# An expert layer with 624 instead of 640 static slots per expert

## The chip, the cores and the metric

The kernel runs on one core of one Trainium2 chip. The metric is the device time of one execution in microseconds, the median of repeated runs. Three timed runs of the kernel before gave 769.81, 770.02 and 771.15 us.

## The reference

Attention with rotary position embedding over 4 batches, 8 heads, 576 positions and 64 dimensions; its output, 2304 rows of 512, is the input of a layer of 8 experts. Each row goes to the two experts with the largest noisy logits and gets the weighted sum of their outputs:

```python
logits = x @ w_gate
noisy_logits = logits + np.log1p(np.exp(x @ w_noise)) * noise
top2 = np.argpartition(-noisy_logits, 2, axis=1)[:, :2]
# top2_w: softmax over the two
for e in range(E):
    for k in range(2):
        mask = top2[:, k] == e
        h = np.maximum(x[mask] @ w1[e], 0.0)          # 512 -> 1024
        out[mask] += top2_w[mask, k, None] * (h @ w2[e])   # 1024 -> 512
```

4608 assignments of rows to experts are made in all, 576 an expert on average; how many an expert gets depends on the data.

## The kernel before

Operations are not written out in their final order. `add` puts each one on a list with its engine, an estimated duration, its dependencies, the buffers that it takes and a priority; `Plan.order` (L199) simulates the engines with these numbers and fixes the order in which instructions are issued. `CFG["dp"]` holds one correction of priority for each operation, by its place in the list.

**Attention and routing** fill the first half. Routing ranks the experts of each token, counts, and scatters each row (512 values as an fp16 high and low part, the weights of the experts, the row numbers) into `xs_rows` in DRAM, which has a region of `REG` rows for each expert; unused slots hold padding whose row number is out of bounds. An expert has `CAP` static slots (L29), in `NJ = CAP // 128` tiles of 128. Experts 0 and 1 are worked on in two parts, slots 0 to 255 before the routing of the last rows is done, and the rest later (`EARLY`, L1164); experts 2 to 7 in one part (`FULL`).

**Each expert** runs through these steps.

- `load_x` (L1172): a transposed load on SyncE's queue brings the rows into `xt` (128 x 8 x slots, fp16: four blocks of 128 dimensions, high and low part), a second load brings `meta` (weights and row numbers), and VectorE scales the weights into `gsc`.
- `weights`, `plan_weights` (L1113, L1144): eight pieces of 512 KB of w1 and w2 are loaded through the staging buffer `wst` and cut into fp16 high and low parts by ScalarE and VectorE. w1 and w2 have two buffers each, for even and odd experts.
- `up` (L1210): for each of 8 blocks of 128 hidden units, 12 products (four blocks of dimensions, three pairs of high and low parts). A product takes one matmul of `w_` columns for a part of up to 512 slots, and two of half the slots (320) for 640. The weights are the stationary operand, `xt` is streamed. ScalarE writes the relu as fp16 (`hh`), VectorE the remainder (`hl`).
- `down` (L1278): for each tile of 128 slots, 24 matmuls of 512 columns (8 blocks of hidden units, three pairs of parts), with the slots as the stationary operand. VectorE scales the sum and adds `prev`, the rows of the output so far, which `fetch` (L1259) has gathered; `spread` (L1306) scatters the result into the output from GpSimd. Gathers of an expert wait for all scatters of the one before.

TensorE's order in the second half is, by and large: first the up blocks of the next expert's block 0, then the down tiles of this expert, then the other seven up blocks of the next one. All matmuls but a few are issued by the helper `mm`, so they carry its line L537 in the trace, and the tile names `ps` (up) and `dn` (down) tell them apart.

**Overflow.** `count` (L1323) compares the largest number of tokens of an expert with `CAP`. Behind the static program a branch handles what is over: it reloads that expert's weights (`reload`) and works on each further 128 slots with `more` (L1431), one step after the other.

Of the kernel before, what the change touches and what calls it, by code (L numbers as in the profile page):

```python
# [12 lines left out]
F16 = mybir.dt.float16  # L13
# [3 lines left out]
OP = mybir.AluOpType  # L17
# [4 lines left out]
NTOK, DM, NE, FF = B * S, 512, 8, 1024  # L22
# [3 lines left out]
QS, VS, XS, MC = 16.0, 64.0, 128.0, 64.0  # L26
PB = 12
GS, W1S, W2S = 256.0, 32.0, 32.0
CAP = 640  # L29
NJ = CAP // 128  # L30
REG = NTOK + CAP
ROW = 1024 + 20
FAR = 1 << 20

# [277 lines left out]
def build(ctx, tc, q, k, v, w_gate, w_noise, noise, w1, w2, tab_d, out):  # L312
    nc = tc.nc
    xs = nc.dram_tensor("xs_rows", (NE * REG, ROW // 2), I32, kind="Internal").ap()

# [10 lines left out]
    pools = {}  # L326
# [209 lines left out]
    def mm(o, w, m, first, last):  # L536
        nc.tensor.matmul(o, w, m, start=first, stop=last, skip_group_check=True)  # L537
# [290 lines left out]
    def masks2():  # L828
# [13 lines left out]
           op0=OP.mult, op1=OP.subtract), prio=25, deps=["wgh"])  # L842
# [45 lines left out]
    def ring(name, bufs):  # L888
        if name not in R_:
            R_[name] = Ring(name, bufs, lambda: None)  # L890
        return R_[name]
# [273 lines left out]
    FULL = ((0, CAP),)  # L1165

    def tiles_of(c0, c1):
        return range(c0 // 128, c1 // 128)

    xbuf, mbuf, gbuf, hbuf, pbuf, ybuf = {}, {}, {}, {}, {}, {}  # L1170

    def load_x(e, c0, c1, deps, pr):  # L1172
        def f():
            s = hid.setdefault(e, dict(meta={}, gsc={}, prev={}, adds=[]))
            if e == 0 and c0 == 0:
                xt = pools["r"].tile([128, 8, c1], F16, name="xe")
            else:
                if "xt" not in s:
                    s["xt"] = pools["l"].tile([128, 8, CAP], F16, name="xt", bufs=2)
                xt = s["xt"][:, :, c0:c1]  # L1180
            s["xt", c0] = xt
            rows = xs[e * REG + c0:e * REG + c1]
            nc.sync.dma_start_transpose(out=xt, in_=rows[:, 0:512].bitcast(F16))  # L1183
            n = (c1 - c0) // 128
            meta = pools["r"].tile([128, NJ, 10], I32, name="meta", bufs=4)
            nc.sync.dma_start(meta[:, 0:n], rows[:, 512:522].rearrange("(j p) m -> p j m", p=128))
            for j in tiles_of(c0, c1):
                s["meta"][j] = (meta, j - c0 // 128)

        def weigh():  # L1190
            s = hid[e]
            n = (c1 - c0) // 128
            meta = s["meta"][c0 // 128][0]
            gsc = pools["r"].tile([128, NJ], F32, name="gsc", bufs=4)
            nc.vector.tensor_scalar(gsc[:, 0:n], meta[:, 0:n, e].bitcast(F32), 1.0 / (XS * W1S * W2S), None, op0=OP.mult)
            for j in tiles_of(c0, c1):
                s["gsc"][j] = gsc[:, j - c0 // 128:j - c0 // 128 + 1]
        if e == 0 and c0 == 0:
            xbuf[e, c0] = Buf(ring("xe", 1))
        else:  # L1200
            if (e, "xt") not in xbuf:
                xbuf[e, "xt"] = Buf(ring("xt", 2))
            xbuf[e, c0] = xbuf[e, "xt"]
        mbuf[e, c0], gbuf[e, c0] = Buf(ring("meta", 4)), Buf(ring("gsc", 4))
        n = (c1 - c0) // 128
        add(("x", e, c0), "SP", 1.1 * n + .4, f, deps=deps + ["swap_right"] + ([] if e == 0 and c0 == 0 else ["swap_left"]),
            uses=[xbuf[e, c0], mbuf[e, c0]], prio=pr, land=1.25 * n + .2)
        add(("wei", e, c0), "DVE", .2, weigh, deps=[("x", e, c0)], uses=[mbuf[e, c0], gbuf[e, c0]], prio=pr + 3)

    def up(e, f, c0, c1, pr):  # L1210
        n = 2 if c1 - c0 > 512 else 1
        w_ = (c1 - c0) // n
        ps_ = Buf(bigs)

        def mms():
            s = hid[e]
            wh, wl = wt[e]["w1"]
            xt = s["xt", c0]
            ps = ps_().rearrange("p (a b) -> p a b", a=2)
            i = 0  # L1220
            for c in range(4):
                for w, x in ((wh, c), (wh, 4 + c), (wl, c)):
                    for a in range(n):
                        mm(ps[:, a, 0:w_], w[:, c, f * 128:(f + 1) * 128], xt[:, x, a * w_:(a + 1) * w_], i == 0, i == 11)
                    i += 1

        def cut(lo):
            s = hid[e]
            if "hh" not in s:
                hid_ = pools["l" if e % 2 else "r"].tile([128, 2, 8, CAP], F16, name="hid", bufs=1)  # L1230
                s["hh"], s["hl"] = hid_[:, 0], hid_[:, 1]
            ps = ps_().rearrange("p (a b) -> p a b", a=2)
            hh = s["hh"][:, f, c0:c1].rearrange("p (a b) -> p a b", a=n)
            if lo:
                hl = s["hl"][:, f, c0:c1].rearrange("p (a b) -> p a b", a=n)
                nc.vector.scalar_tensor_tensor(hl, ps[:, 0:n, 0:w_], 0.0, hh, op0=OP.max, op1=OP.subtract)  # L1236
            else:
                nc.scalar.activation(hh, ps[:, 0:n, 0:w_], AF.Relu)  # L1238
        if e not in hbuf:
            hbuf[e] = Buf(ring("hid%d" % (e % 2), 1))  # L1240
        w = c1 - c0
        a, d = {256: (.28, .33), 384: (.39, .47), 640: (.6, .74)}[w]
        add(("up", e, f, c0), "PE", 12 * w / 2400 + .06, mms, deps=[("x", e, c0)] + wdone[e, "w1"],
            uses=[xbuf[e, c0], wbuf[e, "w1"], ps_], prio=pr)
        add(("hh", e, f, c0), "ACT", a, lambda: cut(False), deps=[("up", e, f, c0)] + (["swap_left"] if e % 2 else ["swap_right"]),
            uses=[ps_, hbuf[e]], prio=pr)
        add(("hl", e, f, c0), "DVE", d, lambda: cut(True), deps=[("hh", e, f, c0)], uses=[ps_, hbuf[e]], prio=pr)

    def ids(e, j, a):
        meta, i = hid[e]["meta"][j]  # L1250
        return meta[:, i, 8 + a:9 + a]
# [24 lines left out]
    behind = [[]]  # L1276

    def down(e, j, pr, prev=True):  # L1278
        dn = Buf(ring("dn", 2), lambda: pools["acc"].tile([128, 512], F32, name="dn"))
        c0 = c_of(e, j)  # L1280

        def mms(part):
            s = hid[e]
            wh, wl = wt[e]["w2"]
            cs = slice(j * 128, j * 128 + 128)
            for f in range(4 * part, 4 * part + 4):
                for a, (h, w) in enumerate(((s["hh"], wh), (s["hh"], wl), (s["hl"], wh))):
                    mm(dn(), h[:, f, cs], w[:, f], f == a == 0, f == 7 and a == 2)
        for part in range(2):
            add(("dn", e, j, part), "PE", 2.59, lambda part=part: mms(part),  # L1290
                deps=[("hl", e, f, c0) for f in range(8)] + wdone[e, "w2"] + ["swap_left"] + ([("dn", e, j, 0)] if part else behind[0]),
                uses=[dn, hbuf[e], wbuf[e, "w2"]], prio=pr + part * .1)

        behind[0] = [("dn", e, j, 1)]
        yb = Buf(ring("y", 2))
        yt = {}

        def scale():
            s = hid[e]
            y = yt[0] = pools["l"].tile([128, 512], F32, name="y", bufs=2)  # L1300
            if prev:
                nc.vector.scalar_tensor_tensor(y, dn(), s["gsc"][j], s["prev"][j], op0=OP.mult, op1=OP.add)  # L1302
            else:
                nc.vector.tensor_scalar(y, dn(), s["gsc"][j], None, op0=OP.mult)

        def spread():  # L1306
            s = hid[e]
            nc.gpsimd.memset(spacer, 0.0)
            i = nc.gpsimd.indirect_dma_start(  # L1309
                out=out, out_offset=bass.IndirectOffsetOnAxis(ap=ids(e, j, 0), axis=0),  # L1310
                in_=yt[0], in_offset=None, bounds_check=NTOK - 1, oob_is_err=False)
            for p in s["adds"]:
                tc.declare_no_dep(i.ins, p, reason="a token has one slot in an expert")
            s["adds"].append(i.ins)
        add(("y", e, j), "DVE", .67, scale, deps=[("dn", e, j, 1), ("wei", e, c0), "swap_left"] + ([("fe", e, j)] if prev else []),
            uses=[dn, yb, gbuf[e, c0]] + ([pbuf[e, j]] if prev else []), prio=pr - 2)
        add(("sp", e, j), "POOL", 1.07, spread, deps=[("y", e, j)] + ([("zero", i) for i in range(18)] if e == 0 else []) +
            ([("sp", e - 1, i) for i in range(NJ)] if e and not (e == 1 and j < 2) else []),
            uses=[yb, mbuf[e, c0]], prio=pr - 2, land=1.4)
# [44 lines left out]
    def go(us):  # L1364
        clk[0] += us

    def ups(e, f):
        up(e, f, *(FULL[0] if e > 1 else EARLY[1]), clk[0])
        go(3.2 if e > 1 else 1.95)

    for f in range(8):
        ups(0, f)
# [113 lines left out]
    with tc.If(some > 0):  # L1486
        for e in range(NE):
            ne = nc.values_load(cnt[0:1, e:e + 1], min_val=0, max_val=NTOK)
            with tc.If(ne > CAP):
                nc.gpsimd.indirect_dma_start(  # L1490
                    out=xs, out_offset=bass.IndirectOffsetOnAxis(ap=cst["tail"][:, e:e + 1], axis=0),
                    in_=pad, in_offset=None)
# [44 lines left out]
```

## Time and profile before

| | |
|---|---|
| median of the timed runs | 770.02 us |
| span of the profiled execution | 772.6 us |
| TensorE (PE) busy | 723.6 us, 94% |
| TensorE weight loads (PEld), overlapping | 497.5 us |
| VectorE (DVE) busy | 415.1 us, 54% |
| ScalarE (ACT) busy | 286.5 us, 37% |
| GpSimd (POOL) busy | 363.9 us, 47% |

Busy time is the time in which at least one instruction of the engine was in work. A row of TensorE's timeline gives the start of the first and the extent of a run of matmuls; matmuls are pipelined, so what one costs is the distance from one start to the next, and a mean duration is longer than that. L12 is line 12 of the kernel. Attention and routing take the span to about 359 us, the experts the rest.

### The profile page before, as it was taken

How to read it: one execution, taken by the hardware profiler on the slowest of the kernel's cores; microseconds unless marked ns; L12 is line 12 of the kernel's file. 1: busy time of each engine (PE TensorE's matmuls, PEld its weight loads, DVE VectorE, ACT ScalarE, POOL GpSimd, SP SyncE). 2: the span in 40 equal slices, each digit the busy share in tenths (PEclk: the TensorE clock that was granted, in tenths of full speed). 3: DMA queues.
4: the chain of work that ended last, by engine and by line, in shares of the span. 5: the costliest groups of instructions: out<-in, count | busy, mean ns of one | idle time of the engine just before them, and what ended most of it. 6: DMA issues, size and time to landing. Idle time of an engine off the chain costs nothing.

```text
span 772.6 us, 18628 instructions
## 1 busy us (share of the span) xinstructions
PE 723.6 (94%) x8094; PEld 497.5 (64%) x8094; DVE 415.1 (54%) x649; ACT 286.5 (37%) x435; POOL 363.9 (47%) x317
## 2 busy tenths in 40 slices
PE   4899998999888899989999999999999999999995
PEld 3677777788777777878555567466475574664752
DVE  6758779877769778777224524334343352342211
ACT  2543546555554665764112313213223042140100
POOL 5799797996515697826431212240331222302311
PEclk9999999999799999999999999999999999999998
DMA  7786565957427594587744894645535537431201
GB/s 156 145 154 127 118 146 122 184 127 157 96 56 170 185 245 117 152 189 258 213 129 146 152 244 136 189 163 144 167 132 165 152 112 194 146 117 55 79 29 39
DMA packets 178812, 112.15 MB, mean 145 GB/s; under 512 B 150431, under 2 KB 155039, under 8 KB 178720
## 3 DMA queue, kind: packets, MB, share of 16 engines
q1 hardware_dynamic: 161632, 72.72, 42.8%
q0 software_dynamic: 9120, 29.03, 10.8%
q10 hardware_dynamic: 7968, 9.12, 3.5%
q8 instruction: 65, 1.06, 0.6%
q14 instruction: 27, 0.22, 0.1%
HBM read 58.57 MB, written 29.22 MB: 114 GB/s over the span
## 4 chain that ended last, share of the span: by engine, by line
PE 51%; issue 11%; DVE 5%; POOL 5%; ACT 4%; DMA 4%; SPq 1%; POOLq 0%; ACTq 0%; DVEq 0%
PE ps L537 25%; PE dn L537 20%; PE acc L537 6%; ACT p L662 2%; POOL p L673 2%; DVE nm L562 2%; POOL out_dram L1309 1%; DMA prev<-out_dram,meta 1%; DMA out_dram<-y,meta 1%; POOL prev L1263 1%; POOL xs_rows L1071 1%; ACT ps L662 1%; ACT xr L778 1%; SPq L1183 1%; DMA xs_rows<-xr,r_ii 1%
## 5 line engine op out<-in xcount | busy, mean ns | idle before, releaser
L537 PE MATMUL dn<-w2h,hid 128*128 128x512 f16 x640 | 191.8, 379 | 0.0
L537 PE MATMUL ps<-xt,w1h 128*128 128x320 f16 (+2 forms) x960 | 177.6, 301 | 0.3 <-DVE nf L1330 0.3
L1309 POOL DMA_INDIRECT out_dram<-y,meta x40 | 53.3, 1332 | 251.7 <-DVE y L1302 209.2
L537 PEld LDWEIGHTS <-hid 128*128 128x128 f16 x960 | 93.9, 98 | 111.9
L1238 ACT ACTIVATE hid<-ps 128x640 f16<-128x640 f32 (+2 forms) x80 | 47.7, 598 | 216.7 <-PE ps L537 216.7
L537 PEld LDWEIGHTS <-w1h 128*128 128x128 f16 x1024 | 100.0, 98 | 41.4 <-issue 0.9
L537 PE MATMUL dn<-w2l,hid 128*128 128x512 f16 x320 | 121.3, 379 | 0.0
L673 POOL TENSOR_TENSOR p<-p 128x1152 f16<-128x1152 f32 (+1 forms) x48 | 100.5, 2108 | 33.3 <-ACT p L662 33.0
L537 PE MATMUL ps<-xt,w1l 128*128 128x320 f16 (+2 forms) x480 | 113.0, 301 | 0.0
L1236 DVE SCALAR_TENSOR_TENSOR hid<-ps,hid 128x640 f16<-128x640 f32 (+2 forms) x80 | 54.9, 690 | 104.6 <-ACT hid L1238 104.5
L662 ACT ACTIVATE p<-ps,pbias 128x576 f32<-128x576 f32 x112 | 79.6, 741 | 72.5 <-PE ps L537 70.8
L562 DVE TENSOR_REDUCE nm<-ps 128x2 f32<-128x576 f32 x128 | 91.2, 750 | 26.2 <-PE ps L537 25.8
L1302 DVE SCALAR_TENSOR_TENSOR y<-dn,gsc,prev 128x512 f32<-128x512 f32 x38 | 28.5, 750 | 135.2 <-PE dn L537 126.0
L537 PE MATMUL ps<-qt,kt 64*128 64x288 f16 (+5 forms) x1200 | 84.9, 262 | 8.4 <-DVE p L669 2.5
L537 PE MATMUL acc<-vb,p 128*128 128x65 f16 (+3 forms) x2040 | 78.1, 194 | 9.5 <-DVE xr L776 8.2
L537 PEld LDWEIGHTS <-p 128*128 128x128 bf16 (+3 forms) x2040 | 70.4, 98 | 22.2 <-issue 17.6
L537 PE MATMUL ps<-kt,qt 64*128 64x288 f16 (+1 forms) x960 | 80.5, 290 | 4.2 <-DVE nm L562 0.9
L537 PEld LDWEIGHTS <-kt 64*128 64x128 f16 (+1 forms) x1200 | 54.1, 97 | 22.4 <-issue 14.1
L537 PEld LDWEIGHTS <-w1l 128*128 128x128 f16 x512 | 50.1, 98 | 19.5
L537 PEld LDWEIGHTS <-qt 64*128 64x128 f16 (+1 forms) x960 | 46.4, 98 | 21.2 <-issue 11.3
L1263 POOL DMA_INDIRECT prev<-out_dram,meta x38 | 39.3, 1034 | 44.1 <-DMA out_dram<-y,meta 25.8
L1071 POOL DMA_INDIRECT xs_rows<-xr,r_ii x36 | 38.5, 1070 | 45.1 <-DVE xr L1054 23.4
(137 smaller groups left out, 810.7 us busy)
## 6 DMA issues: line engine op xcount, KB each, us to landing
wst<-in_moe_w_dram SPq DMA_DIRECT2D x64, 512.0 KB, 4.1
out_dram<-pad ACTq DMA_DIRECT2D x18, 256.0 KB, 2.3
xs_rows<-pad ACTq DMA_DIRECT2D x8, 522.0 KB, 3.9
qin<-in_q_dram SPq DMA_DIRECT2D x16, 256.0 KB, 4.6
qin<-in_k_dram SPq DMA_DIRECT2D x16, 256.0 KB, 4.1
vin<-in_v_dram SPq DMA_DIRECT2D x16, 256.0 KB, 3.7
out_dram<-y,meta POOLq DMA_INDIRECT x40, 4.7
prev<-out_dram,meta POOLq DMA_INDIRECT x38, 3.8
```

What stands on the lines that cost most here:

```text
L537: nc.tensor.matmul(o, w, m, start=first, stop=last, skip_group_check=True)
L562: nc.vector.tensor_reduce(nm()[:, u, :, h], x, axis=AX.X, op=OP.max, negate=True)
L662: nc.scalar.activation(x if way[u] == "P" else halves(whole(u), u, h), x, AF.Exp, bias=pbias, scale=0.125 / (QS * QS))
L673: E.tensor_tensor(b, whole(u), a, op=OP.subtract)
L778: nc.scalar.copy(to, xx)
L1071: i = nc.gpsimd.indirect_dma_start(out=xs, out_offset=bass.IndirectOffsetOnAxis(ap=h["ii"][:, t, a:a + 1], axis=0), in_=r[:, slot(t)], in_ ...
L1183: nc.sync.dma_start_transpose(out=xt, in_=rows[:, 0:512].bitcast(F16))
L1236: nc.vector.scalar_tensor_tensor(hl, ps[:, 0:n, 0:w_], 0.0, hh, op0=OP.max, op1=OP.subtract)
L1238: nc.scalar.activation(hh, ps[:, 0:n, 0:w_], AF.Relu)
L1263: nc.gpsimd.indirect_dma_start(out=prev, out_offset=None, in_=out, in_offset=bass.IndirectOffsetOnAxis(ap=ids(e, j, 1), axis=0))
L1302: nc.vector.scalar_tensor_tensor(y, dn(), s["gsc"][j], s["prev"][j], op0=OP.mult, op1=OP.add)
L1309: i = nc.gpsimd.indirect_dma_start(out=out, out_offset=bass.IndirectOffsetOnAxis(ap=ids(e, j, 0), axis=0), in_=yt[0], in_offset=None, boun ...
```

## The change

`CAP` becomes 624. The number of tiles is rounded up, so it stays at 5, and the regions in DRAM and the buffer `xt` keep 640 rows. What uses the slots themselves gets narrower: the up matmuls of experts 2 to 7 have 312 columns for 320, those of the second part of experts 0 and 1 368 for 384; relu and subtraction handle as many. The fifth down tile has 112 slots: its stationary operand has 112 columns, its result, its scale and its scatter 112 rows. `hid` has rows of 624. The planner is given durations and due times that fit these widths, and the overflow branch begins at 625 tokens.

```diff
-CAP = 640
-NJ = CAP // 128
-REG = NTOK + CAP
+CAP = 624
+NJ = -(-CAP // 128)
+REG = NTOK + NJ * 128
...
     def tiles_of(c0, c1):
-        return range(c0 // 128, c1 // 128)
+        return range(c0 // 128, -(-c1 // 128))
...
     def load_x(e, c0, c1, deps, pr):
+        n = -(-(c1 - c0) // 128)
...
-                    s["xt"] = pools["l"].tile([128, 8, CAP], F16, name="xt", bufs=2)
-                xt = s["xt"][:, :, c0:c1]
+                    s["xt"] = pools["l"].tile([128, 8, NJ * 128], F16, name="xt", bufs=2)
+                xt = s["xt"][:, :, c0:c0 + 128 * n]
             s["xt", c0] = xt
-            rows = xs[e * REG + c0:e * REG + c1]
+            rows = xs[e * REG + c0:e * REG + c0 + 128 * n]
...
-        a, d = {256: (.28, .33), 384: (.39, .47), 640: (.6, .74)}[w]
+        a, d = {256: (.28, .33), 368: (.38, .45), 624: (.585, .72)}[w]
...
     def down(e, j, pr, prev=True):
+        m = min(128, CAP - j * 128)
...
-            cs = slice(j * 128, j * 128 + 128)
+            cs = slice(j * 128, j * 128 + m)
...
-                    mm(dn(), h[:, f, cs], w[:, f], f == a == 0, f == 7 and a == 2)
+                    mm(dn()[0:m], h[:, f, cs], w[:, f], f == a == 0, f == 7 and a == 2)
...
-                nc.vector.scalar_tensor_tensor(y, dn(), s["gsc"][j], s["prev"][j], op0=OP.mult, op1=OP.add)
+                nc.vector.scalar_tensor_tensor(y[0:m], dn()[0:m], s["gsc"][j][0:m], s["prev"][j][0:m], op0=OP.mult, op1=OP.add)
...
-                out=out, out_offset=bass.IndirectOffsetOnAxis(ap=ids(e, j, 0), axis=0),
-                in_=yt[0], in_offset=None, bounds_check=NTOK - 1, oob_is_err=False)
+                out=out, out_offset=bass.IndirectOffsetOnAxis(ap=ids(e, j, 0)[0:m], axis=0),
+                in_=yt[0][0:m], in_offset=None, bounds_check=NTOK - 1, oob_is_err=False)
...
     def ups(e, f):
         up(e, f, *(FULL[0] if e > 1 else EARLY[1]), clk[0])
-        go(3.2 if e > 1 else 1.95)
+        go(3.12 if e > 1 else 1.87)
```

## Rows read from the trace of the kernel before

**Rows 1.** Busy us (instructions) of each engine in stretches of the expert stage.

```profile
core 0: us, PE busy (x) PEld busy (x) DVE busy (x) ACT busy (x) POOL busy (x), PEclk, DMA share, GB/s
358.79:411.75 52.96, 52.96 (x325) 31.80 (x325) 18.05 (x31) 12.49 (x23) 23.20 (x39) 1.00 0.61 177
411.75:452.58 40.83, 40.83 (x207) 19.99 (x205) 16.59 (x21) 9.84 (x13) 9.46 (x13) 1.00 0.81 177
...
507.82:559.80 51.98, 51.98 (x315) 30.54 (x313) 19.85 (x22) 13.65 (x16) 13.79 (x15) 1.00 0.51 155
...
663.80:764.47 100.67, 100.66 (x600) 58.41 (x598) 28.17 (x32) 16.24 (x21) 23.16 (x30) 1.00 0.23 74
764.47:772.60 8.13, 0.00 (x0) 0.00 (x0) 0.75 (x1) 0.00 (x0) 0.99 (x1) 0.75 0.08 26
```

**Rows 2.** Chain of waits, in order of time: start us, us, what.

```profile
390.31 21.45 PE ps L537 x132
...
427.29 9.75 PE ps L537 x60
437.05 15.54 PE dn L537 x72
452.58 29.34 PE ps L537 x216
...
507.82 26.08 PE ps L537 x192
533.90 25.90 PE dn L537 x120
```

**Rows 3.** Groups of weight loads by shape: count, busy us, mean ns, idle before.

```profile
L537 PEld LDWEIGHTS <-hid 128*128 128x128 f16 x960 | 93.9, 98 | 111.9
...
L537 PEld LDWEIGHTS <-kt 64*128 64x128 f16 x960 | 43.0, 95 | 19.0 <-issue 12.5
...
L537 PEld LDWEIGHTS acc<-vf,p 128*128 128x128 f32 x240 | 30.3, 203 | 3.2 <-issue 1.4 <-DVE xr L776 0.9 <-ACT p L662 0.4
...
L537 PEld LDWEIGHTS <-kt 64*64 64x64 f16 x240 | 11.1, 107 | 3.4 <-issue 1.7 <-DVE tmx L589 0.4
```

**Rows 4.** TensorE's timeline in attention: start us, us, engine, what.

```profile
106.90 0.54 PE L537 MATMUL ps<-qt,kt 64*128 64x288 f16 x6
107.28 0.28 PE L537 MATMUL ps<-qlm,cm 64*128 64x288 f16 x2
107.50 1.09 PE L537 MATMUL acc<-vb,p 128*128 128x65 f16 x30
108.52 0.92 PE L537 MATMUL ps<-qt,kt 64*64 64x288 f16 x12
109.28 0.41 PE L537 MATMUL ps<-qlm,cm 64*64 64x64 f16 x6
```

**Rows 5.** Timeline of the last two scales (VectorE) and scatters (GpSimd).

```profile
759.32 0.75 DVE L1302 SCALAR_TENSOR_TENSOR y<-dn,gsc,prev 128x512 f32<-128x512 f32 x1 [4.43 <-PE dn L537]
...
760.35 0.98 POOL L1309 DMA_INDIRECT out_dram<-y,meta  x1 [4.13 <-DVE y L1302]
...
764.50 0.75 DVE L1302 SCALAR_TENSOR_TENSOR y<-dn,gsc,prev 128x512 f32<-128x512 f32 x1 [4.43 <-PE dn L537]
767.00 0.99 POOL L1309 DMA_INDIRECT out_dram<-y,meta  x1 [5.60 <-issue]
```

**Rows 6.** VectorE's timeline between 446 and 480 us.

```profile
448.07 0.75 DVE L1302 SCALAR_TENSOR_TENSOR y<-dn,gsc,prev 128x512 f32<-128x512 f32 x1 [5.05 <-DMA prev<-out_dram,meta]
449.31 0.41 DVE L1195 TENSOR_SCALAR gsc<-meta 128x5 f32<-128x5 f32 x1 [0.50 <-DMA meta<-xs_rows]
...
470.60 1.22 DVE L1137 SCALAR_TENSOR_TENSOR w1l<-wst,w1h 128x1024 f16<-128x1024 f32 x1
```

**Rows 7.** DMA packets: a full tile, expert 0's last, expert 7's last.

```profile
DMA packets 82, 0.29 MB, mean 60 GB/s; under 512 B 16, under 2 KB 16, under 8 KB 80
...
DMA packets 192, 0.46 MB, mean 135 GB/s; under 512 B 24, under 2 KB 24, under 8 KB 192
...
DMA packets 83, 0.19 MB, mean 34 GB/s; under 512 B 40, under 2 KB 40, under 8 KB 80
```

More of the change, by code (lines that the diff above doesn't have):

```diff
@@ L1178, in f @@
                 if "xt" not in s:
-                    s["xt"] = pools["l"].tile([128, 8, CAP], F16, name="xt", bufs=2)
-                xt = s["xt"][:, :, c0:c1]
+                    s["xt"] = pools["l"].tile([128, 8, NJ * 128], F16, name="xt", bufs=2)
+                xt = s["xt"][:, :, c0:c0 + 128 * n]
             s["xt", c0] = xt
-            rows = xs[e * REG + c0:e * REG + c1]
+            rows = xs[e * REG + c0:e * REG + c0 + 128 * n]
             nc.sync.dma_start_transpose(out=xt, in_=rows[:, 0:512].bitcast(F16))
-            n = (c1 - c0) // 128
             meta = pools["r"].tile([128, NJ, 10], I32, name="meta", bufs=4)
@@ L1191, in weigh @@
             s = hid[e]
-            n = (c1 - c0) // 128
             meta = s["meta"][c0 // 128][0]
@@ L1204, in load_x @@
         mbuf[e, c0], gbuf[e, c0] = Buf(ring("meta", 4)), Buf(ring("gsc", 4))
-        n = (c1 - c0) // 128
         add(("x", e, c0), "SP", 1.1 * n + .4, f, deps=deps + ["swap_right"] + ([] if e == 0 and c0 == 0 else ["swap_left"]),
@@ L1301, in scale @@
             if prev:
-                nc.vector.scalar_tensor_tensor(y, dn(), s["gsc"][j], s["prev"][j], op0=OP.mult, op1=OP.add)
+                nc.vector.scalar_tensor_tensor(y[0:m], dn()[0:m], s["gsc"][j][0:m], s["prev"][j][0:m], op0=OP.mult, op1=OP.add)
             else:
-                nc.vector.tensor_scalar(y, dn(), s["gsc"][j], None, op0=OP.mult)
+                nc.vector.tensor_scalar(y[0:m], dn()[0:m], s["gsc"][j][0:m], None, op0=OP.mult)
         def spread():
```

## The prediction

> **What bounds the kernel now.** I first read the busy times by stretch, to see which engine has no idle time where the change acts [rows 1]. [...] VectorE has 19.85 of 51.98 us and ScalarE 13.65. Second, the chain of waits [rows 2]: its pieces follow one another on TensorE without a gap, "ps" for up matmuls and "dn" for down matmuls. The chain of the whole page leaves TensorE at 663.8 us for GpSimd with long "issue" pieces; that is no bound, since rows 1 show TensorE without idle time up to 764.47. So in this stretch a nanosecond off a matmul is a nanosecond off the span, as long as whatever TensorE waits for is still there in time.
>
> Third, what a matmul costs. From rows 2, 120 down matmuls of 512 columns take 25.90 us, 215.8 ns each; 192 up matmuls of 320 columns 26.08 us, 135.8 ns each; the 132 + 60 = 192 up matmuls of 384 columns of experts 0 and 1 take 21.45 + 9.75 = 31.20 us, 162.5 ns each. [...] The 384-column matmul lies on the same line: 135.8 + 64 x 0.417 = 162.5. The price is linear in columns here, and nothing else (weight loads, operand reads) shows in it.
>
> **The change, part by part.** *Up matmuls of experts 2 to 7.* 192 an expert go from 320 to 312 columns: 192 x 8 x 0.417 ns = 0.64 us, six times 3.84 us. *Second part of experts 0 and 1* (slots 256 to 623). 96 matmuls an expert go from 384 to 368 columns: 96 x 16 x 0.417 ns = 0.64 us, twice 1.28 us. The sum is 5.12 us, all in the stretch where TensorE has no idle time. The first 256 slots of experts 0 and 1 don't change.
>
> *The fifth down tile.* Its 24 matmuls still stream 512 columns, so they keep their 215.8 ns: nothing won. Their weight loads get 112 columns where they had 128, and no 112-column load stands in the trace. The bounds are the rows of loads [rows 3]: 128 columns of the same tile 98 ns; 64 columns 107 ns beside 95 ns for 128 columns of the same operand (so the narrower load is the slower one); 128 columns of f32 203 ns. All lie below the 215.8 ns for which the matmul before it runs, and the 98 ns of today are hidden wholly, since the pitch is only about 2.5 ns above the columns. I take zero. Rows 4 say the same for the narrow form: twelve matmuls of 288 columns on 64-column loads take 109.28 - 108.52 = 0.76 us, and six on 128-column loads 107.28 - 106.90 = 0.38 us, 63 ns each both times. The slower load cost nothing even under matmuls of 288 columns. Were the cover gone, the excess would be 9 to 105 ns on 24 x 8 = 192 loads, 1.7 to 20.2 us.
>
> [...]
>
> *Start of the second half.* The second 312 columns start at 624 bytes in a row of xt, not at 640. No row shows that offset for 312 columns. The nearest are the attention matmuls that read vb from a row pitch of 129 elements [rows 4]: 30 of them, of 65 and 64 columns, take 108.52 - 107.50 = 1.02 us, 34 ns each, where the line above gives 29.4. [...] I take zero: those matmuls also need a fresh load every 30 ns, which can account for the excess as well, but I keep 2.7 us for the range.
>
> *ScalarE, VectorE.* Relu and subtraction handle 624 elements for 640; both engines idle more than half of each stretch [rows 1], so this is worth zero. *SyncE, GpSimd.* Transposed loads still fetch five blocks of 128 rows and no DMA is added or taken away; the last scatter of each expert has 112 offsets, and only the very last is at the end of the span, where 16 of 128 offsets off about 1 us (0.99 us, [rows 5]) would be 0.1 us at best. I take zero. The 8.13 us behind the last matmul stay. In them the last scatter begins 767.00 - 764.50 = 2.50 us after its scale began, where the one before it took 760.35 - 759.32 = 1.03 us [rows 5]: 1.47 us for which the profile names no releaser ("issue"). If the shift moves that away, 1.47 us more are won; I don't count on it.
>
> *The planner.* It gets shorter durations and due times that close up by 0.64 us an expert. Everything that begins before the second up matmuls of expert 0 keeps its duration, and their readiness depends on the end of attention, so the order of the first half can't change. In the expert stage near ties can flip.
>
> *What is late next.* TensorE arrives up to 5.12 us earlier, in portions of 0.64 us an expert, and its suppliers are mostly released by its own progress, so they move along. The tightest cover [rows 6]: the first full expert's rows have landed by 449.31 us (VectorE reads their meta data) and TensorE needs them at 452.58 [rows 2]: 3.27 us, of which 1.28 are used up. The weights of expert 3 are cut by 470.60 + 1.22 = 471.82 and needed at 452.58 + 8 x 3.26 = 478.66, 6.8 us. VectorE waited 5.05 us for a gather before the scale at 448.07, but a second accumulator lets TensorE go on. None of these runs out.
>
> So: 772.6 - 5.1 = 767.5 us for the profiled span. The median of the timed runs is 770.02, 2.6 us under the profiled span; the saving is array time, the same in either, so the forecast is 770.02 - 5.12 = 764.9 us.
>
> **The rivals.** (a) *The odd start costs.* Up to 2.7 us come back: 764.9 to 767.6. For it the 34 ns row; against it that the same row has another reason. (b) *A supplier comes late, or the new order is worse.* Place: 427 to 453 us, DMA share 0.81 [rows 1], when expert 2's rows are fetched. It decides once the landing slips by more than 3.27 - 1.28 = 2 us against TensorE; each further microsecond is lost once. 766 to 771. Against it: the same queue released by the same TensorE work. (c) *The 112-column loads are exposed*, the case on the slower side. Place: fifth tile of each expert, 192 loads. To lose more than is won each must cost 5.12 us / 192 = 26.7 ns. At the f32 row's 105 ns of excess it is 764.9 + 20.2 = 785.1. Against it both rows 3 (every bound is under 215.8 ns) and rows 4. [...] (d) *The overflow branch is taken.* It decides at 625 tokens in one expert. The reference on its inputs gives expert 0 just 624, the largest. The transfers of its last tile [rows 7] fit: a full tile has 16 small packets, the last tile of expert 7 (592 - 512 = 80 tokens, 48 rows skipped) 40, that of expert 0 24, so 8 pairs of rows skipped and 112 written: 624 on the chip too. Taken, it would cost at least eight cuts of 1.22 us, 24 x 0.216 and 96 x 0.056 us of matmuls, 20 us: over 785. (e) *The matmul doesn't get shorter with 8 columns less:* 770.0; against it the line through 320, 384 and 512.
>
> **How the numbers follow.** Forecast in full (763.4 to 766) 0.83, (a) 0.06, (b) 0.06, (c) 0.03, (d) 0.01, (e) 0.01. A measurement of this kernel tells about 0.2%, 1.5 us, from no change, so faster means under 768.5: 0.83, all of (a), 0.02 of (b), 0.01 of (c), together 0.92. Within 0.2%: 0.03 of (b) and (e), 0.04. Slower: 0.01 of (b), 0.02 of (c) and (d), 0.04. The range goes from 764.9 - 1.5 (the tail) = 763.4 to 764.9 + 2.7 = 767.6.
>
> **What would show it.** In the chain of the changed kernel 192 up matmuls take 25.44 us (132.5 ns each) and 120 down matmuls still 25.90; the 192 of experts 0 and 1 take 29.9. Load rows of 112 columns between 98 and 203 ns, without a change in the down pitch. TensorE busy through the stretch, its last matmul ending near 759.4 us, a tail near 8.1 us. I am wrong if the down groups exceed 25.90 us (c), if up groups lie between 25.44 and 25.9 (a), or if idle pieces of TensorE appear after 390 us (b).

## The result, and the profile after

The changed kernel is slower: a median of 776.89 us against 770.59 us for the kernel before in the same comparison, a ratio of 1.0083 with a 95% interval of 1.0062 to 1.0104. The forecast was 764.9 us. Measured against 770.59, that is +6.3 us where -5.1 was worked out, so 11.4 us have to be found.

First the part that came as predicted. The chain of waits of the changed kernel (start us, us, what), from the first down matmuls to the end:

```profile
365.38 20.72 PE dn L537 x96
386.11 20.57 PE ps L537 x132
406.68 15.54 PE dn L537 x72
422.21 3.95 PE ps L537 x26
426.16 20.14 DMA xt<-xs_rows
446.35 3.35 PE ps L537 x24
449.70 2.59 PE dn L537 x12
452.29 25.44 PE ps L537 x192
477.73 25.90 PE dn L537 x120
503.63 25.44 PE ps L537 x192
...
757.19 0.76 DVE y L1302
757.98 0.50 POOLq L1485
758.48 0.68 POOL out_dram L1309
```

192 up matmuls take 25.44 us, where they took 26.08 [rows 2]; 120 down matmuls still take 25.90, a fifth of them on the narrow load. Both are the predicted figures to the last digit. 132 of the shorter second parts take 20.57 us for 21.45, which is the predicted 29.9 us for 192. Against the chain of before, two things are new. From 426.16 to 446.35 the chain runs through the DMA that brings expert 2's rows (TensorE works through most of that stretch, as the next rows show), and 24 up matmuls of expert 2 (446.35) stand ahead of the last 12 down matmuls of expert 1 (449.70).

The second thing to look at is what follows TensorE's last matmul. The busy times of the changed kernel by stretch (PE, PEld, DVE, ACT, POOL busy us with instructions; granted clock, DMA share, GB/s):

```profile
411.75:452.58 40.83, 39.16 (x209) 21.72 (x208) 14.15 (x18) 8.86 (x12) 8.23 (x13) 1.00 0.88 148
...
757.19:761.50 4.31, 0.00 (x0) 0.00 (x0) 0.75 (x1) 0.00 (x0) 0.95 (x1) 0.96 0.16 48
761.50:764.40 2.90, 0.00 (x0) 0.00 (x0) 0.00 (x0) 0.00 (x0) 0.00 (x0) 0.50 0.01 3
764.40:774.60 10.20, 0.00 (x0) 0.00 (x0) 0.00 (x0) 0.00 (x0) 0.00 (x0) 0.50 0.00 0
```

In the first row TensorE is busy 39.16 of 40.83 us, where it had no idle time before [rows 1]. In the last row 10.20 us pass with every engine idle and no DMA traffic. The span before ended 8.13 us behind its last matmul [rows 1]; now it is 17.4. What runs there are instructions that the page does not count as busy: GpSimd's closing ones. The trace has them under the two lines that end the kernel (instruction, count, ns least/median/most, first and last start). Before:

```profile
L1533 POOLq DRAIN  x3: 40/107/718, 771.0 to 772.3; - x3
L1486 POOLq INC_SWDGE_SEM  x1: 348/348/348, 770.6 to 770.6; - x1
```

After:

```profile
L1533 POOLq DRAIN  x3: 40/107/9375, 764.4 to 774.3; - x3
L1486 POOLq INC_SWDGE_SEM  x1: 2468/2468/2468, 761.9 to 761.9; - x1
```

INC_SWDGE_SEM took 348 ns and takes 2468; the longest drain took 718 ns and takes 9375. One thing became shorter: the last scale and the last scatter (timeline of the changed kernel, idle time before in brackets):

```profile
757.19 0.75 DVE L1302 SCALAR_TENSOR_TENSOR y<-dn,gsc,prev 112x512 f32<-112x512 f32 x1 [4.43 <-PE dn L537]
758.22 0.95 POOL L1309 DMA_INDIRECT out_dram<-y,meta  x1 [4.13 <-DVE y L1302]
```

The scatter begins 1.03 us after its scale, where it took 2.50 us [rows 5]. So behind the last matmul: 2.12 + 8.66 - 1.47 = 9.3 us more (measured between last matmul and end: 8.10 us before, 17.46 after, +9.36).

The account in the two traces: from the first down matmul to the end of the last one TensorE takes 395.04 us before and 391.93 after, 3.11 less (5.12 saved, 2.01 of idle time); +9.36 behind it; together +6.25, near the measured +6.3. Part of that agreement is luck, since the 2.01 us are those of one execution and change from run to run (5. below). The two profiled spans themselves differ by 2.0 us only (772.6 and 774.6), because the first down matmul starts at 369.4 in one and 365.2 in the other: the half before it has the same instructions in both kernels, and its length varies from execution to execution, by up to 27 us among the chips used here. For that reason the experiments are read from the first down matmul on, and by the closing instructions; the ratios of timed runs stand beside that.

### The profile page after: what moved, and what is told of

Same layout as the page of the kernel before. It is cut to its first block, busy times and chain, and to the rows that moved or that the text cites. A ratio compares the mean times of both kernels' runs of the same rounds, so it can differ in the third digit from the quotient of the medians.

```text
span 774.6 us, 18628 instructions
## 1 busy us (share of the span) xinstructions
PE 714.1 (92%) x8094; PEld 499.6 (65%) x8094; DVE 412.8 (53%) x649; ACT 285.0 (37%) x435; POOL 360.6 (47%) x317
## 3 DMA queue, kind: packets, MB, share of 16 engines
q0 software_dynamic: 9120, 29.03, 11.1%
## 4 chain that ended last, share of the span: by engine, by line
PE 62%; ACT 5%; DVE 5%; DMA 4%; POOL 3%; issue 2%; SPq 1%; POOLq 0%; ACTq 0%; DVEq 0%
PE ps L537 31%; PE dn L537 25%; PE acc L537 6%; DMA xt<-xs_rows 3%; ACT p L662 2%; POOL p L673 2%; DVE nm L562 1%; ACT ps L662 1%; SPq L1185 1%; POOL xs_rows L1071 1%; DMA xs_rows<-xr,r_ii 1%; ACT xr L778 1%; DMA gt<-xr 1%; DVE xr L776 1%; ACT p L666 1%
## 5 line engine op out<-in xcount | busy, mean ns | idle before, releaser
L537 PE MATMUL dn<-w2h,hid 128*128 128x512 f16 (+1 forms) x640 | 192.1, 379 | 1.1 <-DVE y L1302 1.1
L537 PE MATMUL ps<-xt,w1h 128*128 128x312 f16 (+2 forms) x960 | 173.9, 298 | 0.9 <-DMA xt<-xs_rows 0.6
L1309 POOL DMA_INDIRECT out_dram<-y,meta x40 | 50.0, 1251 | 256.6 <-DVE y L1302 217.7
L537 PEld LDWEIGHTS <-hid 128*128 128x128 f16 (+1 forms) x960 | 100.1, 104 | 107.0 <-issue 1.4
L1237 ACT ACTIVATE hid<-ps 128x624 f16<-128x624 f32 (+2 forms) x80 | 46.7, 585 | 235.6 <-PE ps L537 235.6
L537 PE MATMUL dn<-w2l,hid 128*128 128x512 f16 (+1 forms) x320 | 121.3, 379 | 0.0
L537 PE MATMUL ps<-xt,w1l 128*128 128x312 f16 (+2 forms) x480 | 111.5, 298 | 0.0
L1235 DVE SCALAR_TENSOR_TENSOR hid<-ps,hid 128x624 f16<-128x624 f32 (+2 forms) x80 | 53.8, 676 | 99.4 <-ACT hid L1237 99.4
L662 ACT ACTIVATE p<-ps,pbias 128x576 f32<-128x576 f32 x112 | 79.4, 740 | 64.7 <-PE ps L537 63.0
L1302 DVE SCALAR_TENSOR_TENSOR y<-dn,gsc,prev 128x512 f32<-128x512 f32 (+1 forms) x38 | 28.5, 751 | 134.1 <-PE dn L537 119.1
```

Of the source, the lines that this page charges most:

```text
L662: nc.scalar.activation(x if way[u] == "P" else halves(whole(u), u, h), x, AF.Exp, bias=pbias, scale=0.125 / (QS * QS))
L1302: nc.vector.scalar_tensor_tensor(y[0:m], dn()[0:m], s["gsc"][j][0:m], s["prev"][j][0:m], op0=OP.mult, op1=OP.add)
L1309: i = nc.gpsimd.indirect_dma_start(out=out, out_offset=bass.IndirectOffsetOnAxis(ap=ids(e, j, 0)[0:m], axis=0), in_=yt[0][0:m], in_offset= ...
```

## The experiments

Theory R, for the closing stretch, formed after the first four of these runs: the DMAs that GpSimd issues add up to a sum, each with a size by its rows. The DMA at which the sum reaches a limit is held (the 1.47 us ahead of the last scatter of before), and the closing instructions then are short (718 and 348 ns), longer only by a price for each DMA that comes behind it. Where the limit is not reached, they are long (9375 and 2468 ns). The eight scatters of 112 rows add a little less each, so the limit is no longer met. What keeps the sum, and what GpSimd does in the hold, no trace shows. Its rivals: L, the last scatter's shape alone decides; T, each narrow scatter adds its part of the cost; N, the drain is long from some number of narrow scatters on, between two and seven; V, the scatters have nothing to do with it, other parts of the change have. In this section the kernels that start with a have the change, those that start with b have 640 slots.

**1. All scatters 128 rows wide, and only the last one** (a_all128, a_last128). The change stays; the fifth scatter of every expert, or of expert 7 alone, writes 128 rows again.

```diff
+            r = 128 if True else m        # a_last128: if e == NE - 1
-                out=out, out_offset=bass.IndirectOffsetOnAxis(ap=ids(e, j, 0)[0:m], axis=0),
-                in_=yt[0][0:m], in_offset=None, ...
+                out=out, out_offset=bass.IndirectOffsetOnAxis(ap=ids(e, j, 0)[0:r], axis=0),
+                in_=yt[0][0:r], in_offset=None, ...
```

> The changed kernel, but the fifth scatter of every expert has 128 rows again (rows 96 to 127 of its tile are first set to zero on VectorE; the 16 rows too many have row numbers out of bounds and are skipped). Theory L (GpSimd's closing drain is long because the very last scatter has 112 rows): the stretch from the last matmul to the end falls from 17.5 to about 8.1 us, total near 770.6 - 5.1 + 1.7 = 767 us. Theory T (each of the eight short scatters leaves something that the end pays): the same. Theory V (the long drain has nothing to do with the scatters): still 17 us, total near 776.9.

> The changed kernel with 128 rows in the fifth scatter of expert 7 alone; experts 0 to 6 keep 112. L: closing stretch 8.1 us. T: seven eighths of the 9.4 us stay, about 16.3 us. V: 17 us.

With all scatters wide the closing instructions of a_all128 are those of before:

```profile
L1536 POOLq DRAIN  x3: 40/107/718, 762.5 to 763.7; - x3
L1489 POOLq INC_SWDGE_SEM  x1: 348/348/348, 762.1 to 762.1; - x1
```

The stretch behind the last matmul is 8.10 us again, TensorE's part 389.92 us, 5.12 under 395.04, and the kernel is faster than before: 767.69 against 770.6 us, ratio 0.9947 (0.9915 to 0.9979). So the saving is real, V falls, and without the narrow scatters the kernel keeps it. With only the last scatter wide (a_last128) the drain takes 9375 ns and the closing stretch 17.79 us: theory L falls.

**2. Narrow scatters on the kernel before** (b_last112, b_first112, b_all112). The matmuls stay at 640 slots; only the last, the first, or all eight fifth scatters write 112 rows (expert 0 has 624 tokens, the most of all, so the 16 slots left out hold padding).

```diff
+            r = 112 if j == NJ - 1 and e == NE - 1 else 128   # b_first112: e == 0; b_all112: every e
```

> The kernel before, with 112 instead of 128 rows in one scatter, the fifth of expert 7 (its tokens end in row 80 of that tile). L: closing stretch 17.4 us, total 770.6 + 9.3 = 779.9 us. T: 8.1 + 1.2 = 9.3 us, total 771.8. V: unchanged, 770.6.

> The kernel before, with 112 rows in the fifth scatter of expert 0 alone (it has 624 tokens, so none is lost). L: closing stretch 8.1 us. T: 9.3 us. V: 8.1 us.

> The kernel before, with 112 rows in the fifth scatter of all eight experts and nothing else of the change. From the four runs so far: the closing drain is long with eight or seven short scatters and short with none or one. [...] That the scatters need another part of the change for it: 8.1 us and 770.6.

One narrow scatter, wherever it stands, changes nothing: drain 718 ns in both, closing stretch 8.34 and 8.27 us, and for b_last112 a ratio of 0.9986 (0.9945 to 1.0027). All eight bring the whole cost without anything else of the change: 9375 ns, 17.67 us, ratio 1.011 (1.0049 to 1.0171). Between one and eight the cost is not in proportion: T falls.

**3. Where the limit lies** (b_two112, b_three112, b_less1). Two or three narrow scatters; and a kernel with no narrow scatter at all, but one gather of GpSimd left out (the earlier rows of expert 0's fifth tile are not added).

```diff
+            r = 112 if j == NJ - 1 and e < 2 else 128   # b_three112: e < 3
```

```diff
+            if (e, j) == (0, NJ - 1):                   # b_less1, in the gather
+                return
-            if prev:
+            if prev and (e, j) != (0, NJ - 1):          # and in the scale
```

> The kernel before, with 112 rows in the fifth scatter of experts 0 and 1. [...] N with three or more short scatters needed: 0.7 us here and 9.4 us with three.

> The kernel before, with 112 rows in the fifth scatter of experts 0, 1 and 2. [...]

> The kernel before, every scatter with 128 rows, but one software DMA less: the gather of the rows so far for the fifth tile of expert 0 is left out, and that tile is scaled without adding them, so its rows lack what expert 1 gave them early. [...] Theory N (short scatters make the drain long): drain 0.7 us, closing stretch 8.1 us, total unchanged.

The drain of b_two112, then of b_three112, then both rows of b_less1:

```profile
L1534 POOLq DRAIN  x3: 40/107/718, 786.8 to 788.1; - x3
```

```profile
L1534 POOLq DRAIN  x3: 40/107/9375, 784.8 to 794.7; - x3
```

```profile
L1535 POOLq DRAIN  x3: 40/107/9293, 783.8 to 793.7; - x3
L1488 POOLq INC_SWDGE_SEM  x1: 2448/2448/2448, 781.3 to 781.3; - x1
```

Between two and three narrow scatters it goes from nothing to everything (closing 7.99 and 17.75 us). And b_less1 pays in full without one narrow scatter: 17.57 us, ratio 1.0156 (1.0037 to 1.0275) although it does less. So N falls: not the number of narrow scatters, but a sum that falls short. Its closing instructions are 82 and 20 ns shorter than those of after, with 113 DMAs where after has 114: the price of one DMA. At that price after pays for (2468 - 348) / 20 = 106 DMAs more than before, and for (9375 - 718) / 82 = 106 by the drain too. That is somewhat fewer than its 114; why was not tried.

How far the sum reaches: before passes with at most two parts to spare, a part being what a narrow scatter saves (drain 718 ns with two of them, 9375 with three), and a whole DMA is worth three parts or more (9293 ns without one; six or more, by the next experiment, where one DMA makes up for eight narrow scatters). How many parts a whole DMA has, and how many the limit, these runs do not show.

**4. More DMAs on the changed kernel** (a_extra1, a_extra20). If a sum falls short, additional DMAs cure it. Scatters of 128 zero rows into a tensor that nobody reads, behind the gathers of expert 7: one, or ten there and ten behind those of expert 6.

```diff
+            for k in range({6: 0, 7: 1}.get(e, 0) if j == NJ - 1 else 0):   # a_extra20: {6: 10, 7: 10}
+                junk = nc.dram_tensor(f"junk{e}_{k}", (NTOK, DM), F32, kind="Internal").ap()
+                nc.gpsimd.indirect_dma_start(
+                    out=junk, out_offset=bass.IndirectOffsetOnAxis(ap=ids(e, j, 0), axis=0),
+                    in_=pad[:, 0:512].bitcast(F32), in_offset=None, ...
```

> The changed kernel, all eight short scatters kept, with one further software DMA behind the last gathers of expert 7: 128 rows of padding scattered into a DRAM tensor that nobody reads. [...] N: eight short scatters as before, drain 9.4 us, total 777.

> The changed kernel with ten such further software DMAs behind the gathers of expert 6 and ten behind those of expert 7. [...] N: drain 9.4 us or more, as 134 DMAs are to be gone through.

One more transfer (0.16 MB by the page's totals, 29.19 for 29.03: 48 of its 128 rows have numbers out of bounds), and the kernel has 718 and 348 ns again, with a closing stretch of 8.38 us for 17.46: doing more made it shorter. Its ratio to before, 0.9963 (0.9898 to 1.0027), is on the good side, but its interval holds 1; its profiled execution loses 0.87 us in the middle (below). With twenty (a_extra20):

```profile
L1538 POOLq DRAIN  x3: 40/107/2270, 801.2 to 804.1; - x3
L1491 POOLq INC_SWDGE_SEM  x1: 735/735/735, 800.5 to 800.5; - x1
```

and, from GpSimd's timeline of the same run:

```profile
744.84 1.00 POOL L1262 DMA_INDIRECT prev<-out_dram,meta  x1 [5.43 <-issue]
```

The drain is longer than before by the price of (2270 - 718) / 82 = 19 DMAs. In before the last DMA met the limit, so here it was met 19 DMAs before the last. Behind the first of expert 7's gathers 4 gathers, 10 additional scatters and 5 last ones follow, 19. The row of the timeline is that gather, held 5.43 us by "issue"; in a_best_again (below) it is held 2.93 us, by a scatter that has to land. The rest of this run, with 806.12 us the longest of all, is a surprise of its own (last section).

Over all 16 traces the hold and the drain go together. Seven kernels have the hold ahead of the very last scatter, which then begins 2.50 or 2.51 us after its scale, and all of them drain in 718 ns. Six have 1.03 us at their last scatter, and drain in 9293 or 9375 ns. In the other three, a_extra20 and the two runs of 6., the hold stands earlier and the drain grows by the DMAs behind it.

**5. The stall in the middle** (b_flip, a_order). In the changed kernel TensorE waits twice where rival (b) said it would. The rows of after, from its list of waits (us in total, times, longest us) and from TensorE's timeline:

```profile
PE dn L537 <- DVE y L1302: 1.1, 1, 1.1
...
PE ps L537 <- DMA xt<-xs_rows: 0.6, 1, 0.6
```

```profile
443.03 0.38 PE L537 MATMUL dn<-w2h,hid 128*112 128x512 f16 x1 [1.10 <-DVE y L1302]
446.35 0.70 PE L537 MATMUL ps<-xt,w1h 128*128 128x312 f16 x4 [0.57 <-DMA xt<-xs_rows]
```

The second wait is for expert 2's rows, and the order brings it nearer: with 24 up matmuls of expert 2 ahead of 12 down matmuls of expert 1, expert 2's rows are wanted 12 x 0.216 = 2.59 us earlier, beside the 1.28 us saved before it, 3.87 us against a cover of 3.27 [rows 6]. Two kernels part the order from the widths: 640 slots with the new order at that place (b_flip), and 624 slots with the old one (a_order).

```diff
+                 ([("up", 2, 0, 0)] if part and e == 1 and j == NJ - 1 else [])   # b_flip, deps of the down step
```

```diff
-                uses=[dn, hbuf[e], wbuf[e, "w2"]], prio=pr + part * .1)
+                uses=[dn, hbuf[e], wbuf[e, "w2"]], prio=pr + part * .1 - 30 * (e == 1 and j == NJ - 1 and part))   # a_order
```

> The kernel before (640 slots), with expert 2's first 24 up matmuls put ahead of the second half of expert 1's fifth down tile, as the planner does with 624 slots. Theory O (the order takes 2.59 us of the cover of expert 2's rows): these matmuls are due 83.0 - 2.6 = 80.4 us after the first down matmul; the rows landed 79.3 to 82.1 us after it in the profiles so far, so TensorE idles 0 to 1.7 us there, most likely a few tenths or more; nothing at 83.0. Theory W (the widths do it): no idle time here.

> The changed kernel with the old order at that place alone. O: expert 2's first up matmuls are due 83.0 - 1.28 = 81.7 us after the first down matmul, no idle time unless the rows land later than that; 389.9 us from the first down matmul to the last; closing stretch 17.5 us as in the changed kernel. W: idle time as in the changed kernel.

The chain of a_order at that place:

```profile
424.01 15.54 PE dn L537 x72
...
448.90 15.54 PE dn L537 x72
464.44 28.62 PE ps L537 x216
493.06 25.90 PE dn L537 x120
```

The old order is back (72 down matmuls, then 216 up matmuls at one go), and TensorE needs 389.92 us from the first down matmul to the last, 5.12 us under 395.04: no idle time. The new order on 640 slots (b_flip) takes 395.25, 0.21 us more, but they are lost in the first 96 down matmuls (20.93 us for 20.72); expert 2's up matmuls don't wait. Their rows were there: VectorE reads the meta data 79.4 us after the first down matmul, and the matmuls are due at 83.0 - 2.6 = 80.4. So b_flip does not decide between O and W.

Over all runs VectorE reads these meta data between 78.6 and 82.1 us after the first down matmul; the changed kernel wants the rows at 79.1 with the new order, and at 81.7 with the old one. Of the six kernels with the new order two wait for them: after (0.57 us) and a_last128 (0.30). a_all128, a_extra1, a_extra20 and b_flip don't, and neither does any of the ten runs with the old order. So the order takes the margin away, and whether something is lost then is a matter of the run.

The first wait, 1.10 us, stands ahead of the place where the orders part, so the order has no share in it. Matmuls into an accumulator wait for a scale, which itself waited for a late gather (VectorE of after, then the same scale in b_first112):

```profile
442.23 0.75 DVE L1302 SCALAR_TENSOR_TENSOR y<-dn,gsc,prev 128x512 f32<-128x512 f32 x1 [9.37 <-DMA prev<-out_dram,meta]
```

```profile
447.18 0.75 DVE L1302 SCALAR_TENSOR_TENSOR y<-dn,gsc,prev 128x512 f32<-128x512 f32 x1 [6.83 <-DMA prev<-out_dram,meta]
```

Counted from the first down matmul, this scale begins at 77.0 us in after and at 77.2 in b_first112, a kernel of 640 slots, where the kernel before has 72.8: so late a gather is not peculiar to the change. With 640 slots the next down matmul is due at 77.82 us and began at 77.98, 0.16 us lost; with 624 slots it is due 1.28 us earlier, at 76.54, and began at 77.81, 1.27 us lost. Counted from start to start in the same way, the wait for the rows cost the changed kernel 0.72 us; the two make up 1.99 of its 2.01. The 0.87 us of a_extra1 are all of the first kind, the 0.47 of a_last128 of the second. Why the gather lands now early and now late, with the DMA share at 0.88 in after and 0.81 before [rows 1], stays open.

**6. A better kernel** (a_best, twice). The change, the old order at that place, and two additional scatters behind expert 7's gathers. Two, so that the limit is met one scatter before the last, where the 1.47 us lie beside matmuls.

```diff
+            for k in range({6: 0, 7: 2}.get(e, 0) if j == NJ - 1 else 0):
...
+                uses=[dn, hbuf[e], wbuf[e, "w2"]], prio=pr + part * .1 - 30 * (e == 1 and j == NJ - 1 and part))
```

> [...] R: the limit is passed at the last scatter but one, which hides it; last scatter 1.0 us after its scale, closing stretch 8.1 - 1.5 + 0.1 = 6.7 us. No idle time of TensorE between 360 us and its last matmul, so 5.12 us less from the first down matmul to the last. Total 770.6 - 5.1 - 1.4 = 764.1 us. N: 17 us of closing stretch, 774.

> The same kernel as the one with two further software DMAs and the restored order, on another chip job, since its comparison with the kernel before was too wide. R: closing stretch 6.7 to 6.9 us, 389.9 us from the first down matmul to the last at the full clock, ratio to the kernel before (770.6 - 5.1 - 1.3) / 770.6 = 0.9917. If the expert stage wins nothing beyond the changed kernel with full scatters (ratio 0.9947): 0.9947.

The last two scatters in the second of these runs (timeline), and its closing instructions:

```profile
765.66 0.99 POOL L1314 DMA_INDIRECT out_dram<-y,meta  x1 [5.62 <-issue]
...
769.36 0.95 POOL L1314 DMA_INDIRECT out_dram<-y,meta  x1 [2.64 <-DVE y L1307]
```

```profile
L1538 POOLq DRAIN  x3: 40/107/800, 773.6 to 774.9; - x3
L1491 POOLq INC_SWDGE_SEM  x1: 368/368/368, 773.2 to 773.2; - x1
```

The hold ("issue") is now ahead of the last scatter but one; the last waits for its scale alone. One DMA more is paid for than before (800 - 718 = 82 ns, 368 - 348 = 20 ns), and the closing stretch is 6.9 us in both runs, the shortest of all. The ratios are 0.9854 (0.9717 to 0.9991) and 0.9885 (0.9817 to 0.9953). Worked out from the parts it should be 770.59 - 5.12 - 1.2 = 764.3 us, a ratio of 0.9918, which lies in both intervals; so does 0.9947, the ratio of the changed kernel with full scatters. In the two profiled executions TensorE needs 391.00 and 390.71 us from the first down matmul to the last, where 389.9 was expected; the difference lies in the first 96 down matmuls (21.80 and 21.51 us for 20.72), and behind them no idle time is left. The kernel beats the one before, by at least 0.47% in the second comparison; whether it beats a_all128 these runs do not say.

## Why the prediction was wrong, point by point

*What bounds the kernel.* Right for the stretch that was read: TensorE without idle time, and each nanosecond off a matmul came off that stretch. But the bound was asked for only up to 764.47 us.

*The up matmuls.* Right: 5.12 us predicted, 395.04 - 389.92 = 5.12 measured in the two kernels of the change without idle time (a_all128, a_order). By rows 2 a column costs (215.8 - 135.8) / 192 = 0.417 ns, and 512 of them leave 2.5 of the 215.8 ns over; the price holds at the new width: (26.08 - 25.44) us / (192 x 8) = 0.417 ns.

*The fifth down tile, rival (c).* Right at zero. The two groups of loads in the changed kernel, by shape (busy us, mean ns, idle before):

```profile
L537 PEld LDWEIGHTS <-hid 128*128 128x128 f16 x768 | 75.2, 98 | 89.1
L537 PEld LDWEIGHTS <-hid 128*112 128x112 f16 x192 | 25.0, 130 | 17.9 <-issue 1.4
```

A load of 112 columns takes 130 ns, inside the bounds of 98 to 203. Those loads stay under the 215.8 ns of a matmul, and 120 down matmuls keep their 25.90 us.

*The start of the second half, rival (a).* Right at zero: 25.44 us per 192 is the line without an addition, and no run shows the 2.7 us that the range allows for this start, an estimate (4.6 ns on each of 576 matmuls, the 34 ns of rows 4 less the 29.4 of the line). Rivals (d) and (e) did not come about: the chain has no additional tiles, and the matmul is shorter by 8 columns.

*SyncE, GpSimd.* **This step failed.** I counted the GpSimd DMAs that are issued (none added, none taken away) and the time of the last one (0.1 us at best), and wrote that the 8.13 us behind the last matmul stay. The price hung on a sum over all 114 of them, which the eight narrower scatters make too small for a limit that the kernel before just reached (with two of them it is still reached, with three no longer). The term put at zero is 9.36 us. No rival had this sum; those that could end slower than before, (b), (c) and (d), had other causes. The trace of before did hold the hint, and I passed it: the 1.47 us ahead of the very last scatter for which the profile names no releaser [rows 5]. I noted it as something that might be won if it moved; it did go away, and with it gone the closing instructions took 2.12 + 8.66 us more. A hold without a releaser was taken as loss to be had, without asking what would take its place.

*The planner, rival (b).* Half right. I wrote that near ties can flip and named the place (427 to 453 us), the cover (3.27 us) and the point of decision; I gave it 0.06 and counted only the 1.28 us of earlier arrival. The flip itself adds 2.59 us, and 3.87 is over the cover. The greater part of the loss is another: of the gathers I wrote that a second accumulator lets TensorE go on, from one trace in which VectorE waited 5.05 us. With a gather that came 4 us later than in that trace, as in other runs of either kernel, and with the 1.28 us of earlier arrival, TensorE did wait. The two were worth 2.01 us in the profiled execution (1.27 and 0.72) and 0 to 0.87 in the other kernels of the change, so by themselves they would have left 765 to 767 us, inside the range.

## What to carry to other kernels

When a change alters the number or the width of the transfers that GpSimd issues itself, look at the end of the trace behind the last data transfer, at instructions that count as busy on no engine, before calling that stretch constant; here eight scatters that were narrower by 16 rows cost 9.4 us there, and one useless transfer won 9.1 of them back. For a hold for which the profile names no releaser, find out what takes its place before it is put down as a cost or a gain: here 1.47 us of it went away, and 10.78 us of closing instructions came. A step whose duration changes by 2.5% can still swap places with its neighbour in a planned order; price the swap (2.59 us here), not the 2.5%. A cover that is read from one trace holds for that execution: the gather above came 4 us later in others.

## What was not expected of the hardware

The closing cost of GpSimd's DMAs, 82 + 20 = 102 ns for each DMA that is paid for and 10.8 us for 106 of them, is such a thing, and so is its disappearance when the sum reaches the limit, for 1.47 us at one DMA.

The other is in a_extra20. TensorE's busy time in stretches of that run (columns as above), around its two groups of ten additional scatters, one about every 1.3 us, and then its list of waits from 680 us on, which has this row alone:

```profile
686.00:696.00 10.00, 10.00 (x77) 7.25 (x76) 4.24 (x5) 2.61 (x4) 7.87 (x8) 1.00 0.78 286
696.00:706.00 10.00, 6.18 (x26) 2.49 (x25) 1.36 (x2) 1.97 (x3) 5.13 (x7) 0.75 0.53 173
...
756.00:766.00 10.00, 4.17 (x14) 1.28 (x14) 0.81 (x1) 0.69 (x1) 6.07 (x8) 0.65 0.30 115
```

```profile
PE ps L537 <- issue: 9.8, 14, 1.7
```

In 696 to 706 us it is busy 6.18 us, in 756 to 766 us 4.17. The waits have no releaser ("issue"). The mean granted clock goes from 1.00 to 0.75 and 0.65 in those stretches. TensorE waits first: its first wait of the first group ends at 696.70 us, where a matmul still takes 0.29 us, and at 701.41 one of the same shape takes 0.47. From the first down matmul to the last TensorE needs 407.94 us instead of 389.92; the waits make 9.8 of these 18.0 us. The rest was not taken apart; longer matmuls like the one of 0.47 us are in it. The scatters began at 689.9 and 751.2 us, 6.4 and 4.6 us ahead of the first wait of each group. What TensorE waited for stays open. With one or two such scatters nothing of the kind is seen.
